# Delta-rule attention with a two-layer expert, float32 on one core: the front of the program reordered as a whole

## The chip, the cores and the metric

The kernel runs on one core of one Trainium2 chip. The metric is device time of one execution in microseconds (us). Three runs of the kernel before took 591.02 (median), 589.74 and 594.14 us.

## The reference, cut to what matters

```python
# q, k, v: (4 batches, 8 heads, 768 steps, 48); beta: (4, 8, 768)
k_n = k / (norm(k, axis=-1) + 1e-06)
for t in range(768):                       # state: 48 x 48 per head
    y[t] = q[t] @ state
    state += beta[t] * outer(k_n[t], v[t] - k_n[t] @ state)
x = y.transpose(0, 2, 1, 3).reshape(3072, 384)
h = x @ w_in                               # 384 x 2048
g = where(h >= 1, h, where(h <= -1, 0, (h + 1) ** 2 / 4))
return g @ w_out                           # 2048 x 384
```

## The kernel before, in words

**Tiling.** The 768 steps are cut into 12 chunks of 64, two chunks are a pair (G = 0 to 5), and all 32 heads of a chunk are worked on together. Inside a chunk the recurrence becomes a triangular system of 64 x 64 per head. For chunk g, `gram_k` makes the products of the keys with each other and `gram_q` those of queries and keys, of which only one triangle may stay (the mask). The systems of a pair are laid out one to a partition (`lanes`), scaled by beta and the squared norms of the keys, and inverted: `solve` does blocks of 16 x 16 on VectorE in 15 steps of a product and a subtraction, `unlanes` transposes the result back, and TensorE joins the blocks to 32 and 64 (`merge16_a`, `merge16_b`, `merge32`). The state is then carried from chunk to chunk by `chain_r` (correct the values by the old state), `chain_u` (apply the inverse), `chain_y` (the outputs y), and `chain_d` (the new state).

**The expert.** Its hidden width of 2048 is cut into 16 tiles f. `up` makes h for the 512 tokens of a pair (nine float32r products of 512 columns, since operands are split in a high and a low part and three of four combinations are kept), ScalarE and VectorE form g and split it (`rest`), and `down` adds g times the second weight into four banks. Each weight tile arrives packed and is unpacked once, in the first pair: `grow` and `cast` on ScalarE, `shift`, `join` and `low` on VectorE.

**Front and loop.** Nothing of the expert can start until the first chunk is through its chain. This front is the code from `load_k(0)` down to `spare[:] =`. After it, `items` runs over the pairs and tiles, with the attention work of later chunks threaded in. The first pair is done in halves at first: its first `HALF` = 6 items use chunk 0 alone (256 columns).

**What sets the order.** The order is written by hand (`manual_schedule`): each engine takes its instructions in the order of the code. Two tables of letters place small tasks: `FRONT`, one string for each stage of the front, and `FILL`, one for each item. A comma separates the points in a stage or item. `A` is the next ScalarE step of unpacking (`grow` or `cast`), `D` the next one of VectorE (`shift`, `join`, `low`), `L` the next step of the second pair's `lanes`, `S` one of its solve, `s`, `t` a scaling of values by key norms, `m`, `M` one mask product, `w` the load of the next weight tile, `F` one product of zeros by `dense` (TensorE gets work whose result is not used).

`stage` issues a stage's products, then the letters ahead of the comma, then the evictions:

```python
def stage(pieces, n):
    evicts = products(*pieces)
    codes = FRONT[n].split(",")
    do(codes[0])
    finish(evicts)
    do(codes[1])
```

Loads go out on SyncE's queue in the order of the code; at most eight of them are under way, since each waits for the one eight places ahead to have landed.

Of the kernel before, what the change touches and what calls it, by code (L numbers as in the profile page):

```python
# [19 lines left out]
DF = 2048  # L20
FT = DF // 128
WARM = 8
IDLE = 18
DENSE = (8, 4, 8, 10)
HALF = 6
PASSES = ((0, 0), (0, 1), (1, 0))
# [14 lines left out]
def delta_rule_moe(ctx: ExitStack, tc: tile.TileContext, kqa, kqb, kv, beta, w, out):  # L41
# [14 lines left out]
    nc = tc.nc  # L56
# [9 lines left out]
    const = ctx.enter_context(tc.tile_pool(name="const", bufs=1))  # L66
    sb = ctx.enter_context(tc.tile_pool(name="sb", bufs=2))
# [13 lines left out]
    def half(x):  # L81
        return slice(x * H, x * H + H)
# [38 lines left out]
    def weight_loads(n0, n1, q=nc.sync):  # L121
# [7 lines left out]
    beta_sb = const.tile([P, NS, 32], F32, name="beta_sb")  # L129
# [16 lines left out]
    for c0, base, step, n in ((0, -H, -C, NP), (NP, -C - H - NP, C, NP), (C, -C, C, H)):  # L146
        x = perm[:, 0:C].rearrange("c (a f l) -> c a f l", f=2, l=H)[:, :, :, c0:c0 + NP] if c0 < C else perm[:, C:P].rearrange("c (a f l) -> c a f l", f=2, l=H)
# [12 lines left out]
    nc.vector.memset(warm.bitcast(F32), 0.0)  # L160
    warm_ps = ps.tile([P, 512], F32, name="o1")

    def dense(n):
        for _ in range(n):
            nc.tensor.matmul(warm_ps, warm[:, 0:P], warm, start=True, stop=True)  # L165
    dense(WARM)
    mask = const.tile([P, C], F32, name="mask")
    nc.gpsimd.memset(mask, 1.0)
    for r in (0, C):
        nc.gpsimd.affine_select(out=mask[r:r + C], in_=mask[r:r + C], pattern=[[1, C]], base=0,  # L170
                                channel_multiplier=-1, compare_op=ALU.is_gt, fill=0.0)
# [59 lines left out]
    def gram_k(g):  # L231

        x, b_ = KE.pop(g) if g in KE else K[g], banks(C)
        for j in range(H):
            for e, f in quarters():
                k, o = x[f * C:f * C + D, e * H + j, :], (1 - e) * C
                nc.tensor.matmul(b_[f][o:o + C, j], k, k, start=True, stop=True)  # L237

        def evict():
            for f in range(2):  # L240
                nc.scalar.copy(out=(GE[g - 2] if g in (2, 3) else GG[:, g % 2])[:, half(f)], in_=b_[f])
        return evict

    def gram_q(g):

        x, b_ = Q[g], banks(C)
        for j in range(H):
            for e, f in quarters():
                r, o = slice(f * C, f * C + D), other(e, f) * C
                nc.tensor.matmul(b_[e][o:o + C, j], K[g][r, e * H + j, :], x[r, (1 - f, 1)[e], e * H + j, :], start=True, stop=True)  # L250

        def moved():
            for o in range(2):
                yield x[o * C:o * C + C, o, 0:H], b_[0][o * C:o * C + C], slice(o * C, o * C + C)
            yield x[:, 0, H:NU], b_[1], slice(0, P)

        def evict():
            def raw():
                for a, b, r in moved():
                    nc.scalar.copy(out=a, in_=b)  # L260

            def masks(copied=False):
                for a, b, r in moved():
                    nc.vector.tensor_tensor(out=a, in0=a if copied else b, in1=mask[r, None, :].broadcast_to([r.stop - r.start, H, C]), op=ALU.mult)
                    yield

            def later():
                raw()
                for a, b, r in moved():
                    for c in range(r.start, r.stop, C):  # L270
                        y = x[c:c + C, 0 if r.stop - r.start > C else c // C, (0, H)[r.stop - r.start > C]:(H, NU)[r.stop - r.start > C]]
                        nc.gpsimd.affine_select(out=y, in_=y, pattern=[[0, H], [1, C]], base=0, channel_multiplier=-1,  # L272
                                                compare_op=ALU.is_gt, fill=0.0)
            return (raw, masks(True)) if g < 2 else lambda: run(masks()) if g < 4 else later()
        return evict

    def norms(n, out):

        y = sb.tile([P, 32], F32, name="y0")
        r = sb.tile([P, 32], F32, name="r1")  # L280
        nc.scalar.activation(out=y, in_=n, func=AF.Sqrt, bias=tiny)
        nc.vector.reciprocal(out=r, in_=y)
        nc.vector.tensor_tensor(out=r, in0=r, in1=n, op=ALU.mult)
        nc.vector.tensor_tensor(out=r, in0=r, in1=y, op=ALU.add)
        nc.vector.tensor_scalar(out=out, in0=r, scalar1=0.5, scalar2=1e-6, op0=ALU.mult, op1=ALU.add)
        return r

    def scale_v(g):

# [5 lines left out]
    S = {}  # L295
    ZT = XT[:, :, :, 0:32]

    def lanes(G):

        for g in range(2):  # L300
            x = GE[g] if G == 1 else GG[:, g]
            for u in (half(0), half(1)) if (G, g) == (0, 1) else (slice(0, NU),):
                for r in (0, C):
                    (nc.scalar.copy if G else nc.vector.tensor_copy)(out=x[r:r + 32, u, 32:64], in_=x[r:r + 32, u, 0:32])
            if G == 1:
                nc.scalar.copy(out=GD[:, g], in_=x[:, :, 32:64])
            yield
# [6 lines left out]
                nc.gpsimd.memset(Xf[:, 256 * s:256 * s + 256:17], 1.0)  # L314
        if G == 0:
            nc.gpsimd.memset(ZT[:, :, :, 16:32], 0.0)
        nc.vector.transpose(out=A, in_=(GD if G == 1 else GG[:, :, :, 32:64]).rearrange("p g u t -> p t (g u)"))
        yield
        n = sb.tile([P, 32], F32, name="N2")
        r = norms(A.rearrange("l j t -> l (j t)")[:, 0:1024:33], n)  # L320
        gm = S["gm"] = sb.tile([P, 32], F32, name="gm")
        nc.vector.reciprocal(out=r, in_=n)
        nc.vector.tensor_tensor(out=gm, in0=r, in1=beta_sb[:, G, :], op=ALU.mult)
        nc.vector.tensor_tensor(out=gm, in0=gm, in1=r, op=ALU.mult)
        N = S["N", G] = sb.tile([P, 32], F32, name="N3")
        if G:
            nc.vector.transpose(out=N, in_=n)
        yield
        if G >= WHOLE:
# [9 lines left out]
        if G == 0:  # L339
            nc.vector.transpose(out=N, in_=n)  # L340
        yield

    def solve(G):

# [297 lines left out]
    def run(gen, n=99):  # L642
        for _ in range(n):
            if next(gen, 0) == 0:
                break
# [62 lines left out]
    tasks.update({"m": raws[0][1], "M": raws[1][1], "S": solve(1), "U": unlanes(1)})  # L708
# [241 lines left out]
```

## Time and profile before

| | |
|---|---|
| median of 3 runs | 591.02 us |
| the profiled execution | 590.3 us, span 588.6 us, 1.7 us around it |
| TensorE matmul busy | 569.0 us (97%) |
| VectorE, ScalarE, GpSimd busy | 405.2 (69%), 327.5 (56%), 54.5 us (9%) |
| mean granted clock of TensorE | 0.992 of full speed |
| first product of the expert | starts at 51.00 us |

PE is TensorE, PEld its weight loads, DVE VectorE, ACT ScalarE, POOL GpSimd, SP SyncE. A row names line, engine, operation, output <- input, shape, and in brackets the idle time ahead of it and what ended that. "issue" is waiting for nothing that the profile shows.

### The profile page before, as it was taken

To read this page: it belongs to the slowest core of one execution; us is meant where nothing else is said; L and a number is where in the kernel's file an instruction comes from. 1 tells how busy PE (TensorE), PEld (TensorE's weight loads), DVE (VectorE), ACT (ScalarE), POOL (GpSimd) and SP (SyncE) were. 2 spreads that over 40 slices of the span, in tenths; PEclk is the share of its full clock that TensorE was granted. 3 is DMA by queue.
4 is the path that set the end of the run, shared out by engine and by line. 5 is a ranking of instruction groups with operands and counts; after the bars stand their busy time and mean duration, and the time that the engine had idled before them with its cause. 6 is when DMAs were issued, how large, how long until landed. Compare 5 with 4: busy or idle time off the path is not lost.

```text
span 588.6 us, 21697 instructions
## 1 busy us (share of the span) xinstructions
PE 569.0 (97%) x9585; PEld 493.3 (84%) x9585; DVE 405.2 (69%) x828; ACT 327.5 (56%) x587; POOL 54.5 (9%) x91
## 2 busy tenths in 40 slices
PE   8998899999999999999999999999999999999996
PEld 7776788788978888888888888888888888898986
DVE  5977999963689864599954599954599955333332
ACT  4648886358644575545575445575445564454443
POOL 6200010000000500010400011300011300000000
PEclk9979999999999999999999999999999999999999
DMA  5673766200333111134011134011133000020001
GB/s 147 199 253 138 213 212 192 77 4 10 95 81 100 31 32 39 39 97 114 24 33 41 37 103 119 16 30 45 36 106 96 1 3 16 15 55 1 0 2 53
DMA packets 32302, 42.77 MB, mean 73 GB/s; under 512 B 7056, under 2 KB 26768, under 8 KB 32208
## 3 DMA queue, kind: packets, MB, share of 16 engines
q1 hardware_dynamic: 31216, 40.41, 24.0%
q8 instruction: 75, 1.23, 0.9%
q0 software_dynamic: 576, 0.57, 0.4%
q10 hardware_dynamic: 416, 0.39, 0.2%
q14 instruction: 19, 0.16, 0.1%
HBM read 34.47 MB, written 4.72 MB: 67 GB/s over the span
## 4 chain that ended last, share of the span: by engine, by line
PE 47%; issue 22%; DVE 14%; DMA 6%; SPq 6%; ACT 2%; POOL 1%; POOLq 0%; DVEq 0%; ACTq 0%
PE h L738 18%; PE o L753 17%; DMA wt<-in_w_dram 4%; PE ch L534 3%; PE ch L237 2%; DVE s L893 2%; PE ch L508 2%; DVE pr L366 1%; DVE A L368 1%; DVE glo L857 1%; PE ch L250 1%; SPq L595 1%; PE ch L492 1%; DMA KV<-in_kv_dram 1%; DVE wt L208 1%
## 5 line engine op out<-in xcount | busy, mean ns | idle before, releaser
L738 PE MATMUL h<-xb,wt 128*128 128x512 f32 (+1 forms) x918 | 223.0, 386 | 5.1 <-DVE s L893 2.0
L753 PE MATMUL o<-wt,ghi 128*128 128x384 f32 x768 | 200.0, 342 | 0.1
L738 PEld LDWEIGHTS h<-xb,wt 128*128 128x128 f32 x918 | 161.8, 188 | 38.9 <-DVE s L893 3.4
L753 PEld LDWEIGHTS o<-wt,ghi 128*128 128x128 f32 x768 | 137.2, 188 | 7.0 <-issue 0.3
L753 PE MATMUL o<-wt,glo 128*128 128x384 f32 x384 | 129.4, 337 | 0.4 <-DVE glo L857 0.4
L856 ACT CAST ghi<-s 128x512 fp32r<-128x512 f32 (+1 forms) x102 | 60.8, 597 | 120.4 <-DVE s L893 107.8
L893 DVE SCALAR_TENSOR_TENSOR s<-s,h 128x512 f32<-128x512 f32 (+1 forms) x102 | 66.3, 650 | 77.1 <-ACT s L891 76.8
L877 ACT ACTIVATE s<-h,half 128x512 f32<-128x512 f32 (+1 forms) x102 | 67.4, 661 | 53.8 <-PE h L738 53.6
L857 DVE TENSOR_TENSOR glo<-s,ghi 128x512 fp32r<-128x512 f32 (+1 forms) x102 | 66.8, 654 | 39.5 <-ACT ghi L856 39.3
L753 PEld LDWEIGHTS o<-wt,glo 128*128 128x128 f32 x384 | 72.1, 188 | 1.0 <-DVE glo L857 1.0
L891 ACT ACTIVATE s<-s 128x512 f32<-128x512 f32 (+1 forms) x102 | 62.2, 610 | 2.2
L368 DVE TENSOR_TENSOR A<-A,pr 128x30 f32<-128x30 f32 (+14 forms) x120 | 45.4, 378 | 4.4
L366 DVE TENSOR_TENSOR pr<-A 128x30 f32<-128x30 f32 (+14 forms) x120 | 43.4, 362 | 2.2
L272 POOL TENSOR_SCALAR_AFFINE_SELECT Q<-Q 64x512 f32<-64x512 f32 x32 | 21.7, 680 | 117.4 <-ACT Q L260 116.0
L165 PE MATMUL o<-wx 128*128 128x512 f32 x87 | 27.8, 464 | 1.5 <-DVE tiny L175 1.5
L534 PEld LDWEIGHTS ch<-Q,SU 64*64 64x64 f32 (+3 forms) x1056 | 22.4, 135 | 3.7 <-ACT ghi L856 1.5
L534 PE MATMUL ch<-Q,SU 64*64 64x64 f32 (+3 forms) x1056 | 24.7, 222 | 0.0
L331 POOL TENSOR_SCALAR_AFFINE_SELECT A<-A 128x1024 f32<-128x1024 f32 x4 | 5.6, 1390 | 191.5 <-DMA xb<-X 148.1
L165 PEld LDWEIGHTS o<-wx 128*128 128x128 f32 x87 | 18.2, 220 | 5.6 <-DVE tiny L175 1.5
L626 DVE TENSOR_TENSOR SU<-ch,SU 48x384 f32<-48x384 f32 x36 | 19.9, 554 | 3.9 <-PE ch L607 3.5
L590 DVE TENSOR_TENSOR X<-ch,X 128x128 fp32r<-128x128 f32 x20 | 5.8, 292 | 23.5 <-ACT xb L586 22.5
L517 ACT COPY SU<-ch 64x384 f32<-64x384 f32 (+1 forms) x30 | 14.3, 476 | 7.0 <-PE ch L508 6.7
(168 smaller groups left out, 559.5 us busy)
## 6 DMA issues: line engine op xcount, KB each, us to landing
wt<-in_w_dram SPq DMA_DIRECT2D x16, 768.0 KB, 5.6
out_dram<-wx SPq DMA_DIRECT2D x44, 96.0 KB, 2.2
KV<-in_kv_dram SPq DMA_DIRECT2D x36, 96.0 KB, 2.4
KV<-in_kv_dram SPq DMA_DIRECT2D x72, 48.0 KB, 2.3
KV<-in_kv_dram SPq DMA_DIRECT2D x12, 192.0 KB, 2.7
xb<-X SPq DMA_DIRECT2D x60, 32.0 KB, 2.0
K<-in_kqb_dram SPq DMA_DIRECT2D x12, 128.0 KB, 2.6
Q<-in_kqb_dram SPq DMA_DIRECT2D x12, 128.0 KB, 2.7
```

What stands on the lines that cost most here:

```text
L165: nc.tensor.matmul(warm_ps, warm[:, 0:P], warm, start=True, stop=True)
L272: nc.gpsimd.affine_select(out=y, in_=y, pattern=[[0, H], [1, C]], base=0, channel_multiplier=-1, compare_op=ALU.is_gt, fill=0.0)
L366: nc.vector.tensor_tensor(out=pr, in0=A[:, 0:n, j:j + 1].broadcast_to([P, n, m]), in1=A[:, j:j + 1, j + 1:32].broadcast_to([P, n, m]), op= ...
L368: nc.vector.tensor_tensor(out=A[:, 0:n, j + 1:32], in0=A[:, 0:n, j + 1:32], in1=pr, op=ALU.add)
L534: nc.tensor.matmul(yy[i][o * C:o * C + C, e, p], SF[rows, u:u + C], w_[rows, x, k, :], **how)
L738: nc.tensor.matmul(h[:, cols(bs)], WT[f][:, 0, x, k * P:(k + 1) * P], XB[G][:, y, k, cols(bs)], start=(n == 0), stop=(n == 8))
L753: nc.tensor.matmul(oacc[G, k], (ghi, glo)[x][:, k * P:(k + 1) * P], WT[f][:, 1, y, :], start=(new and n == 0), stop=(left[G, b] == 0 and n ...
L856: nc.scalar.copy(out=ghi[:, c], in_=s[:, c])
L857: nc.vector.tensor_tensor(out=glo[:, c], in0=s[:, c], in1=ghi[:, c], op=ALU.subtract)
L877: nc.scalar.activation(out=s[:, c], in_=h[:, c], func=AF.Relu, bias=mid, scale=0.5)
L891: nc.scalar.activation(out=s[:, c], in_=s[:, c], func=AF.Square)
L893: nc.vector.scalar_tensor_tensor(out=s[:, c], in0=s[:, c], scalar=1.0, in1=h[:, c], op0=ALU.min, op1=ALU.max)
```

## The change

It touches the front, the twelve mask products of chunks 0 to 3, and five weight loads; all products of the expert and of the chain stay.

- **First norms.** The first pair's scale, beta / (norm + 1e-6)^2, was made by a square root on ScalarE, a Newton step, and two reciprocals. Now `squares` makes it from n + 2e-6 sqrt(n) + 1e-12 with one reciprocal; the norm itself, which scales the values, follows later (`norms_first`). Of the first four evictions of `gram_k` two go to VectorE, and two of its lane copies to ScalarE.
- **Masks.** All products with the mask tile on VectorE become selects on GpSimd, as chunks 4 to 11 have them. Those of chunks 0 and 1 stand behind two memsets in the front. Chunks 2 and 3 get a copy on ScalarE ahead of their selects.
- **Second pair's lanes** (transpose, norms, scaling) move to later places of VectorE's queue.
- **Loads.** The values of chunk 1 go ahead of weight tiles 2 to 4. Tiles 2 to 6 each get a `gate`, one element set by VectorE, behind which the load has to wait.
- **Products of zeros.** Ahead of the first merge 38 of 280 columns stand instead of 18 of 512; between the stages 5, 5, 5, 5 and 4 instead of 1, 12, 2, 5 and 3. The names of accumulators are dealt in another order, so that the first `up` no longer shares a bank with `chain_d`.

```diff
-IDLE = 18
+IDLE = 38
 FRONT = (
-    "sAwFALs,", "FLFFFDFFLFFFFF,F", "FFDD,S", "mFFFFFmm,", "AFFFD,AAw", ",", "DA,Dt")
+    "AFFFFFA,", "FFFFF,sswD", "FFFFF,D", "FFFFF,wDL", "AFFFF,AwD", "Dw,", "LLAw,ASDt")
...
+            if gate:
+                nc.vector.memset(RAW[f][0:1, 0, 0:1], 0.0)
             q.dma_start(out=RAW[f].bitcast(I32), in_=w.bitcast(I32)[:, f])
...
     load_kv(0)
-    weight_loads(2, 5)
     load_kv(1)
...
-            return (raw, masks(True)) if g < 2 else lambda: run(masks()) if g < 4 else later()
+            return (raw, select) if g < 2 else later
...
+    def squares(n, gm, out):
+        y = sb.tile([P, 32], F32, name="y0")
+        d = sb.tile([P, 32], F32, name="r1")
+        nc.scalar.activation(out=y, in_=n, func=AF.Sqrt, bias=tiny)
+        nc.vector.tensor_scalar(out=gm, in0=n, scalar1=1e-12, scalar2=None, op0=ALU.add)
+        nc.vector.tensor_copy(out=d, in_=n)
+        nc.vector.scalar_tensor_tensor(out=gm, in0=y, scalar=2e-6, in1=gm, op0=ALU.mult, op1=ALU.add)
+        nc.vector.reciprocal(out=gm, in_=gm)
+        nc.vector.tensor_tensor(out=gm, in0=gm, in1=beta_sb[:, 0, :], op=ALU.mult)
+        S["first"] = y, d, out
...
-    dense(IDLE)
+    dense(IDLE, 280)
...
     for x in (SF, SZ):
         nc.gpsimd.memset(x, 0.0)
+    for _, select in raws:
+        select()
     run(unlanes(0))
+    norms_first()
```

**VectorE between the first solve and the first merge.** Before, from the end of `unlanes` (the transposes into `XT`) to the subtraction that ends `merge16_b` (`XT<-XT,ch`), with the second pair's norms between:

```order
L394 STREAM_TRANSPOSE XT<-A 128x16x32
L396 STREAM_TRANSPOSE XT<-A 128x16x32
...
L317 STREAM_TRANSPOSE A<-wt_144 128x1024
...
L282 RECIPROCAL r_694<-y_693 128x32
...
L338 TENSOR_TENSOR A_712<-A,gm 128x256 x2
L424 TENSOR_TENSOR XT<-XT,ch 128x16x16
L425 STREAM_TRANSPOSE GG<-XT 128x16x32
```

The changed program there:

```order
L411 STREAM_TRANSPOSE XT<-A 128x16x32
L413 STREAM_TRANSPOSE XT<-A 128x16x32
L272 RECIPROCAL r_559<-y_462 128x32
L273 TENSOR_TENSOR r_559<-r_559,r_463 128x32
L274 TENSOR_TENSOR r_559<-r_559,y_462 128x32
L275 TENSOR_SCALAR N_458<-r_559 128x32
L358 STREAM_TRANSPOSE N_460<-N_458 128x32
L441 TENSOR_TENSOR XT<-XT,ch 128x16x16
L442 STREAM_TRANSPOSE GG<-XT 128x16x32
```

The second pair's transpose and norms have left this place; five small steps of the first pair's own norm stand there.

**VectorE around the first product of the expert.** Before, between the low part of y (`xb<-ch,xb`) and the work that follows (`KV` is the scaling of values, `wt<-xb,wt` is `low`):

```order
L561 TENSOR_TENSOR xb<-ch,xb 128x3x64 x2
L208 TENSOR_TENSOR wt_860<-xb,wt_860 128x2x384
L195 TENSOR_SCALAR xb<-xb 128x768
L292 TENSOR_TENSOR KV<-KV,N_461 128x384 x2
```

The changed program there:

```order
L578 TENSOR_TENSOR xb<-ch,xb 128x3x64 x2
L272 RECIPROCAL r_965<-y_964 128x32
...
L339 STREAM_TRANSPOSE N_815<-N_813 128x32
L350 TENSOR_TENSOR A_975<-A,gm 128x256 x2
L125 MEMSET wt_980 1x1
L372 TENSOR_TENSOR pr<-X,A_975 128x30
L374 TENSOR_TENSOR X<-X,pr 128x2x15
L191 TENSOR_SCALAR xb<-xb 128x768
L301 TENSOR_TENSOR KV<-KV,N_460 128x384 x2
```

The second pair's norms and scaling now come here; `low` of tile 0 has moved ahead of the first row.

**GpSimd in the front of the changed program** (`A`, `SU` and `wt` are buffers set to zero):

```order
L368 MEMSET A 128x1024
L719 MEMSET SU 128x1552
L719 MEMSET wt_165 128x1536
L262 AFFINE_SELECT Q<-Q 64x512 x8
L321 MEMSET X 128x512
```

The row of eight selects is new; before, the memset of `X` followed the two memsets.

## Rows read from the trace of the kernel before

**Rows 1.** The page's part 1: busy us (share of span) xinstructions.

```profile
PE 569.0 (97%) x9585; PEld 493.3 (84%) x9585; DVE 405.2 (69%) x828; ACT 327.5 (56%) x587; POOL 54.5 (9%) x91
```

**Rows 2.** Windows: busy us of PE, PEld, DVE, ACT, POOL, then PEclk, DMA, GB/s.

```profile
30.00:31.00 1.00, 0.71 (x52) 0.72 (x56) 1.00 (x2) 0.31 (x1) 0.00 (x0) 0.51 0.78 197
36.00:37.00 1.00, 1.00 (x3) 0.46 (x2) 0.97 (x4) 0.00 (x0) 0.00 (x0) 0.57 1.03 302
...
55.00:60.00 5.00, 3.92 (x200) 3.47 (x200) 5.00 (x9) 4.97 (x9) 0.00 (x0) 1.00 0.23 61
```

**Rows 3.** Timeline of DVE in the front: start us, us, instruction, [idle before].

```profile
7.96 2.24 DVE L304 COPY GG<-GG 32x512 f32<-32x512 f32 x6 [4.31 <-ACT GG L241]
10.23 2.01 DVE L317 STREAM_TRANSPOSE A<-GG 128x1024 f32<-128x1024 f32 x1
...
15.45 0.19 DVE L355 TENSOR_TENSOR pr<-X,A 128x30 f32<-128x30 f32 x1
...
24.21 0.43 DVE L391 TENSOR_TENSOR A<-X,gm 128x256 f32<-128x256 f32 x1
...
27.41 1.05 DVE L396 STREAM_TRANSPOSE XT<-A 128x512 f32<-128x512 f32 x1
...
31.07 0.35 DVE L282 RECIPROCAL r<-y 128x32 f32<-128x32 f32 x1
...
33.45 0.76 DVE L338 TENSOR_TENSOR A<-A,gm 128x256 f32<-128x256 f32 x2
34.12 0.42 DVE L424 TENSOR_TENSOR XT<-XT,ch 128x256 f32<-128x256 f32 x1
```

**Rows 4.** Timeline of PE in the front and the first items.

```profile
21.57 4.38 PE L165 MATMUL o<-wx 128*128 128x512 f32 x18
...
28.60 0.43 PE L419 MATMUL ch<-wt,XT 32*32 32x16 f32 x28 [0.75 <-ACT wt L412]
30.29 1.57 PE L419 MATMUL ch<-wt,XT 32*32 32x16 f32 x100 [1.26 <-issue]
31.79 5.35 PE L165 MATMUL o<-wx 128*128 128x512 f32 x12
37.07 1.20 PE L436 MATMUL h<-XT,GG 32*32 32x32 f32 x64
...
42.05 1.15 PE L508 MATMUL o<-KV,XT 64*64 64x48 f32 x64
...
48.18 0.31 PE L539 MATMUL ch<-Q,wt 64*64 64x64 f32 x5 [1.47 <-issue]
...
62.00 1.20 PE L436 MATMUL ch<-XT,GG 32*32 32x32 f32 x64 [0.53 <-DVE XT L424]
```

**Rows 5.** Timeline of POOL in the front, and in pair 2.

```profile
16.36 1.40 POOL L702 MEMSET SU<- 128x1552 f32 x1
...
285.99 2.89 POOL L272 TENSOR_SCALAR_AFFINE_SELECT Q<-Q 64x512 f32<-64x512 f32 x4 [4.69 <-ACT Q L260]
```

**Rows 6.** Timeline of DVE: one subtraction alone, and one beside those selects.

```profile
198.75 0.22 DVE L368 TENSOR_TENSOR A<-A,pr 128x30 f32<-128x30 f32 x1
...
288.23 0.71 DVE L368 TENSOR_TENSOR A<-A,pr 128x30 f32<-128x30 f32 x1
```

**Rows 7.** Timeline of DVE around the first items.

```profile
49.18 0.62 DVE L561 TENSOR_TENSOR xb<-ch,xb 128x192 fp32r<-128x192 f32 x2 [1.57 <-ACT xb L556]
49.72 0.95 DVE L208 TENSOR_TENSOR wt<-xb,wt 128x768 fp32r<-128x768 f32 x1
...
55.53 0.95 DVE L208 TENSOR_TENSOR wt<-xb,wt 128x768 fp32r<-128x768 f32 x1
...
61.53 0.42 DVE L424 TENSOR_TENSOR XT<-XT,o 128x256 f32<-128x256 f32 x1
```

**Rows 8.** Waits of PE, 50 to 150 us: us in total, times, longest.

```profile
PE h L738 <- DVE s L893: 2.0, 3, 1.1
```

**Rows 9.** The chain that ended last, in order of time: start, us, what.

```profile
29.67 9.21 DMA wt<-in_w_dram
```

More of the change, by code (lines that the diff above doesn't have):

```diff
@@ L161, in delta_rule_moe, with dense @@
     warm_ps = ps.tile([P, 512], F32, name="o1")
-    def dense(n):
+    def dense(n, cols=512):
         for _ in range(n):
-            nc.tensor.matmul(warm_ps, warm[:, 0:P], warm, start=True, stop=True)
+            nc.tensor.matmul(warm_ps[:, 0:cols], warm[:, 0:P], warm[:, 0:cols], start=True, stop=True)
     dense(WARM)
[L167 to L171, printed above, removed]
     mid = const.tile([P, 1], F32, name="half")
@@ L240, in evict @@
             for f in range(2):
-                nc.scalar.copy(out=(GE[g - 2] if g in (2, 3) else GG[:, g % 2])[:, half(f)], in_=b_[f])
+                (nc.vector.tensor_copy if f and g < 2 else nc.scalar.copy)(out=(GE[g - 2] if g in (2, 3) else GG[:, g % 2])[:, half(f)], in_=b_[f])
         return evict
@@ L260, in raw, with select @@
                     nc.scalar.copy(out=a, in_=b)
[L262 to L268, printed above, removed]
+            def select():
                 for a, b, r in moved():
@@ L273, in later, with newton @@
                                                 compare_op=ALU.is_gt, fill=0.0)
-            return (raw, masks(True)) if g < 2 else lambda: run(masks()) if g < 4 else later()
-        return evict
+            def later():
+                raw()
+                select()
+            return (raw, select) if g < 2 else later
+        return evict
+    def newton(r, n, y, out):
+        nc.vector.reciprocal(out=r, in_=y)
+        nc.vector.tensor_tensor(out=r, in0=r, in1=n, op=ALU.mult)
+        nc.vector.tensor_tensor(out=r, in0=r, in1=y, op=ALU.add)
+        nc.vector.tensor_scalar(out=out, in0=r, scalar1=0.5, scalar2=1e-6, op0=ALU.mult, op1=ALU.add)
     def norms(n, out):
@@ L281, in norms @@
         nc.scalar.activation(out=y, in_=n, func=AF.Sqrt, bias=tiny)
[L282 to L285, printed above, removed]
-        return r
+        newton(r, n, y, out)
+        return r
+    def squares(n, gm, out):
[8 more added lines that the diff above has]
+        S["first"] = y, d, out
     def scale_v(g):
@@ L303, in lanes @@
                 for r in (0, C):
-                    (nc.scalar.copy if G else nc.vector.tensor_copy)(out=x[r:r + 32, u, 32:64], in_=x[r:r + 32, u, 0:32])
+                    (nc.scalar.copy if G or u == half(0) else nc.vector.tensor_copy)(out=x[r:r + 32, u, 32:64], in_=x[r:r + 32, u, 0:32])
             if G == 1:
@@ L316, in lanes @@
             nc.gpsimd.memset(ZT[:, :, :, 16:32], 0.0)
+        n = sb.tile([P, 32], F32, name="N2")
+        diag = A.rearrange("l j t -> l (j t)")[:, 0:1024:33]
+        gm = S["gm"] = sb.tile([P, 32], F32, name="gm")
+        N = S["N", G] = sb.tile([P, 32], F32, name="N3")
         nc.vector.transpose(out=A, in_=(GD if G == 1 else GG[:, :, :, 32:64]).rearrange("p g u t -> p t (g u)"))
         yield
[L319 to L326, printed above, removed]
+        if G == 0:
+            squares(diag, gm, n)
+        else:
+            r = norms(diag, n)
+            nc.vector.reciprocal(out=r, in_=n)
+            nc.vector.tensor_tensor(out=gm, in0=r, in1=beta_sb[:, G, :], op=ALU.mult)
+            nc.vector.tensor_tensor(out=gm, in0=gm, in1=r, op=ALU.mult)
             nc.vector.transpose(out=N, in_=n)
@@ L338, in lanes, with norms_first @@
             nc.vector.tensor_tensor(out=A16[:, s], in0=A[:, b, b], in1=gm[:, b, None].broadcast_to([P, 16, 16]), op=ALU.mult)
-        if G == 0:
-            nc.vector.transpose(out=N, in_=n)
         yield
+    def norms_first():
+        y, d, n = S["first"]
+        r = sb.tile([P, 32], F32, name="r1")
+        newton(r, d, y, n)
+        nc.vector.transpose(out=S["N", 0], in_=n)
     def solve(G):
@@ L659, in delta_rule_moe @@
     spare += START
-    acts = [(f, grow) for f in range(2)] + [x for f in range(FT) for x in ((f + 2, grow), (f, cast)) if x[0] < FT]
+    acts = [(f, grow) for f in range(2)] + [x for f in range(FT) for x in (((f + 2, grow), (f, cast)) if f > 1 else ((f, cast), (f + 2, grow))) if x[0] < FT]
     vecs = [x for f in range(FT + 1) for x in ((f, shift), (f, join), (f - 1, low)) if 0 <= x[0] < FT]
@@ L702, in delta_rule_moe @@
         nc.gpsimd.memset(x, 0.0)
+    for _, select in raws:
+        select()
     run(unlanes(0))
+    norms_first()
     one_ = lambda f, *a: [lambda: f(*a)]
@@ L707, in delta_rule_moe @@
     stage(one_(merge16_b, 0), 1)
-    tasks.update({"m": raws[0][1], "M": raws[1][1], "S": solve(1), "U": unlanes(1)})
+    tasks.update({"S": solve(1), "U": unlanes(1)})
     stage(one_(merge32, 0, None, True), 2)
@@ L713, in delta_rule_moe @@
     stage(both(chain_d, 0), 6)
-    spare[:] = START[0:2] + START[4:6]
+    spare[:] = START[0:4]
     oacc, gs = {}, {}
```

12 lines of the change are left out of this document (6 added, 6 removed).

## The prediction, made before the changed kernel ran

> **What bounds the kernel now.** The page's engine line comes first: TensorE is busy for 569.0 of 588.6 us [rows 1]. The rest, some 20 us, is ahead of the first product of the expert or in holes, so the time is the moment when the first `up` starts (51.00 us, the table) plus what TensorE then loses. Second, the timeline of TensorE in the front [rows 4]: there most of its "busy" is products of zeros, so the busy share says nothing about whether the front can be shorter. Third, what the real products wait for: lanes, the solve (15.45 to 24.21), `unlanes` (to 27.41 + 1.05 = 28.46), all on VectorE [rows 3], then merges and chain. Fourth, the windows: from 55 to 60 us VectorE is busy 5.00 of 5 us and TensorE 3.92 [rows 2]. So in the first items, too, VectorE sets the pace, and work that the change puts on it there is paid in full.
>
> **The change part by part.**
>
> *Norms and lanes.* The six lane copies cost VectorE 2.24 us, 0.37 each [rows 3]. Two go to ScalarE, two evictions come the other way; halves that run beside each other gain me 0.6 us (an estimate; bounds 0 and the two copies' 0.75). From the end of the transpose (10.23 + 2.01 = 12.24) to the solve's first step are 3.2 us of small steps [rows 3]. A reciprocal (0.35, as the second pair's) and about four steps of 0.2 with their turns go: 1.2 us, bounds 0 and 2.0. The solve then starts at 15.45 - 1.8 = 13.7.
>
> *Masks.* Eight selects on GpSimd now follow the two memsets. One memset took 1.40 us beside the solve [rows 5]; after two of them from about 14 us the selects start near 17.3 and last 8 x 2.89/4 = 5.8 us [rows 5], so they fall inside the solve. This is the part that speaks against the change: one subtraction of the solve took 0.22 us alone and 0.71 beside such a select [rows 6]. A step of the solve comes on average every (24.21 - 15.45)/30 = 0.29 us. In 5.8 us go 5.8/0.72 = 8 slowed steps, which need 8 x 0.29 = 2.3 us otherwise: 3.4 us are lost. Bounds: 0, if the selects are late enough to miss the solve, and 8 x (0.71 - 0.22) = 3.9; I take 3.4, as rows 6 show this pair of operations itself. The solve ends at 13.7 + 8.8 + 3.4 = 25.9, `unlanes` (28.46 - 24.21 = 4.25) at 30.1, later than before.
>
> *First merge.* `merge16_b` started 0.15 us after `unlanes` and worked 0.43 + 1.57 us, with a hole of 1.26 between [rows 4]. Now it runs from 30.25 to 32.25. Behind it, before, the subtraction waited on VectorE until 34.12 behind the second pair's transpose, norms and scaling [rows 3], and `merge32` until 37.07 behind twelve products of zeros, 5.35 us at about half of the clock [rows 4, 2]. Both covers go: subtraction and transpose (0.42 and about 0.7) end near 33.4, five products of 280 columns cost 5 x 280/6144 x 5.35 = 1.2 us beside them. `merge32` starts at about 33.45: **+3.6 us**. The 38 products ahead of it are 10640 columns for 9216, 4.38 x 1.155 = 5.1 us from 21.57, so they end near 26.7 and stand ahead of nothing that could run. They would matter only if the selects cost nothing: `merge16_b` could not start before 28.2, so at most 2.1 more is to be had there. Between the later stages 1400 columns replace 1024 to 2560: nothing, since the evictions they cover are unchanged.
>
> *The two holes.* Inside `merge16_b` TensorE stood 1.26 us, inside `chain_y` 1.47 us, with "issue" [rows 4]: no semaphore, hence no cause in the profile. Both stand where weight tiles stream (0.78 to 1.03 of the DMA engines busy [rows 2]). The values now come first and tiles singly, so I expect the second hole nearly gone, **+1.0** (bounds 0 and 1.47), and the first to return in part, **-0.4** (0 and -1.26). The Trainium skill, "Runtime: NRT & Kernel Launch", section "Instruction fetch mechanics", says that an engine's sequencer fetches its next block of instructions while it executes, and that this is mostly hidden. By that rule neither hole is late instructions that lighter loads would bring sooner, and no row here shows which it is; that outcome is the third rival.
>
> *VectorE after y.* The second pair's norms (31.07 to 33.45 without the 0.5 of a `shift`: 1.9), its scaling (0.76) and two solve steps (0.4) now follow y at once, where `low` of tile 0 (0.95 [rows 7]) stood: 1.9 + 0.76 + 0.4 - 0.95 = 2.1. Before, from y's last piece to the second pair's merge subtraction passed 61.53 - 49.80 = 11.7 us of a full VectorE [rows 7, 2]. So that subtraction, and with it the second pair's `merge32`, comes later against y: **-2.1** (bounds -1.2, if the solve steps and part of the scaling merely move, and -3).
>
> *A hole ahead of that merge.* `low` of tile 2 ended at 56.48 and `merge32` began at 62.00, with TensorE filling what lay between [rows 7, 4]. With `low` earlier, its products are through and TensorE stands, by about 5.5 less 0.8 for the rest of the item, 4.7 us. The wait itself is in the term before. But after TensorE had stood for most of 27.8 to 30.3 us, its clock at 30 us was 0.51, the lower level of 1.2 GHz, and at 36 still 0.57 [rows 4, 2]. So it ran about six microseconds at half. If it falls again I take **-2.3**: six microseconds at half clock lose at most 3.2, but VectorE is the bound for part of them. Bounds 0 and -3.2.
>
> *Later waits.* TensorE waited three times for VectorE's `s` in the first items, 2.0 us together [rows 8]. These go when unpacking is less bunched: **+1.9** (0 and 2.0).
>
> *Loads and gates.* Five one-element memsets are nothing on VectorE. Queued on SP behind each gate are the next tiles and then the later chunks' loads, needed tens of microseconds on. When tile 2 lands is a rival.
>
> **Sum.** 3.6 - 0.4 + 1.0 - 2.1 - 2.3 + 1.9 = 1.7 us gained. Against the profiled execution, 590.3, that is 588.6. The median of the three runs is 0.7 above it, the lowest 0.6 below; I add 0.3 and forecast **588.9 us**. With all terms at their ends the sum goes from about -4 to +7, but ends do not coincide.
>
> **Rivals.**
>
> *(a) VectorE's crowding costs less.* The clock stays up in the hole (TensorE still works in it, as it did from 55 to 60 us), or the selects miss the solve. For it: 0.71 is one subtraction's duration, and the memset beside the solve slowed nothing [rows 5, 3]. Against: rows 6 are this very pair. The first gives 588.9 - 2.3 = 586.6, the second 588.9 - 2.1 = 586.8, both 584.5. Chance 0.30.
>
> *(b) Slower: a late tile 2.* Its gate comes after the first merge and two scalings of values, about 34.5 us, and ScalarE's `grow` of it stands in the queue ahead of the evictions of `chain_y`, due near 44 (48.18 less 3.2 and 1.0). `grow` takes 0.9, so it costs time as soon as the tile needs over 43.1 - 34.5 = 8.6 us from its issue, and every microsecond beyond delays y and all that follows. For it: one weight tile took 9.21 us [rows 9]; the DMA engines were full at 36 us [rows 2]. Against: then several tiles shared the engines, now tiles go singly. At 13 us the price is 4.4: 593.3, slower than before; above 10.5 us the gain is gone. Chance 0.10.
>
> *(c) The holes stay.* Both "issue" holes return whole: 1.0 lost in `chain_y`, 0.9 more in `merge16_b`, so the gain is -0.2 and the time 590.8, no change. For it: nothing in the profile ties them to loads but the place. Against: there are stretches of as many instructions without one. Here the change does not do what its order of loads says. Chance 0.18; by the rule of the Trainium skill above it would be the likeliest for `chain_y`.
>
> **How the numbers follow.** Forecast 0.42 (587.5 to 590.2), (a) 0.30 (584 to 587.5), (c) 0.18 (590.2 to 592), (b) 0.10 (592 to 597). The range 584.8 to 592.5 leaves out the quickest tenth and most of (b). What a measurement can tell from no change is 1%, 5.9 us: faster is below 585.1, which only the lower end of (a) reaches with a little from the forecast's other bounds, 0.15; slower is above 596.9, (b)'s far end, 0.05; within 1%, 0.80.
>
> **What would show it.** In the profile after: subtractions and products of the solve at 0.7 us beside selects from about 17 to 23 us, and 0.2 before and behind (right for the mask term; at 0.2 throughout it falls); `merge32` at about 33.5 and `chain_u` 3 us earlier than 42.05; the first `up` near 47 us; a wait of TensorE for `XT` of 4 to 5 us ahead of the second pair's `merge32`, near 60 us, and a granted clock of 0.5 in the windows behind it; no hole inside `chain_y`; no wait of TensorE for `s` in the first items. Wrong it is if `grow` of tile 2 waits for a load, if a new "issue" hole of over 1 us opens in the front, or if the first `up` comes early and the end does not follow, since then the loss lies in the items and not in the terms above.

## The result: slower by 1.3%, and the profile after

Four runs of the changed kernel took 597.92 us (median; 596.64 to 603.07), four of the kernel before (the three named above and one more) 592.58. The ratio is **1.0127** (1.0086 to 1.0168): some 7.5 us slower by the ratio (the two medians alone are 5.3 us apart), where 1.7 us faster was forecast and 592.5 was the range's end. The profiled execution took 599.1 us, span 597.4, mean granted clock 0.974 (before 590.3, 588.6, 0.992). Runs of one kernel spread by up to 10 us here, so times are compared by ratios to the kernel before, each with its 95% interval; a trace says where time lies in one execution.

`s` is VectorE's step in forming g, one for each item, so its times tell how far the expert has come. The first is 4.9 us later than before (58.61 for 53.73), and the fourteenth still 4.5. The fifteenth is 9.2 later, and the last 8.8: a second loss falls near 125 us. The windows show both. Columns are busy us of PE, PEld, DVE, ACT, POOL, then granted clock, DMA share, GB/s.

```profile
30.00:35.00 5.00, 4.85 (x136) 3.72 (x135) 2.40 (x9) 1.21 (x3) 0.00 (x0) 0.52 0.35 93
35.00:40.00 5.00, 4.62 (x71) 3.20 (x70) 4.94 (x11) 1.17 (x3) 0.00 (x0) 0.50 0.73 224
40.00:45.00 5.00, 5.00 (x73) 3.78 (x71) 0.59 (x1) 1.87 (x4) 0.00 (x0) 0.50 0.38 145
45.00:50.00 5.00, 4.90 (x101) 3.68 (x101) 2.37 (x7) 1.99 (x4) 0.00 (x0) 0.77 0.11 12
...
60.00:65.00 5.00, 5.00 (x158) 4.52 (x160) 4.65 (x8) 3.16 (x6) 0.00 (x0) 0.57 0.30 99
120.00:125.00 5.00, 4.27 (x180) 3.21 (x168) 3.59 (x7) 3.40 (x7) 0.00 (x0) 1.00 0.20 57
125.00:130.00 5.00, 3.09 (x10) 3.09 (x11) 2.64 (x5) 1.05 (x2) 0.00 (x0) 0.58 0.02 3
130.00:135.00 5.00, 5.00 (x79) 3.76 (x79) 0.00 (x0) 2.15 (x4) 1.42 (x3) 0.74 0.00 0
```

TensorE runs at 1.2 GHz from 30.2 to 47.3 us, where before it came back at 36.9 [rows 2]; and twice more in the expert, from 57.5 to 64.3 and from 125.8 to 132.6. On VectorE the steps of the solve, the end of `unlanes`, the first merge's subtraction and the second pair's:

```profile
17.63 0.29 DVE L372 TENSOR_TENSOR pr<-X,A 128x126 f32<-128x126 f32 x1
17.96 0.71 DVE L374 TENSOR_TENSOR X<-X,pr 128x126 f32<-128x126 f32 x1
...
23.02 0.68 DVE L372 TENSOR_TENSOR pr<-X,A 128x110 f32<-128x110 f32 x1
23.73 0.28 DVE L374 TENSOR_TENSOR X<-X,pr 128x110 f32<-128x110 f32 x1
...
29.37 1.04 DVE L413 STREAM_TRANSPOSE XT<-A 128x512 f32<-128x512 f32 x1
...
33.91 0.42 DVE L441 TENSOR_TENSOR XT<-XT,ch 128x256 f32<-128x256 f32 x1 [2.43 <-PE ch L436]
...
66.85 0.41 DVE L441 TENSOR_TENSOR XT<-XT,o 128x256 f32<-128x256 f32 x1
```

Eight steps take 0.68 to 0.71 us beside the selects, and 0.3 just before and behind them. The timeline of TensorE answers to [rows 4]:

```profile
28.06 1.59 PE L422 MATMUL ch<-XT,GG 32*32 32x16 f32 x128 [0.71 <-DVE XT L411]
29.59 2.01 PE L166 MATMUL o<-wx 128*128 128x512 f32 x5
...
31.97 1.89 PE L436 MATMUL ch<-wt,XT 32*32 32x16 f32 x124 [0.15 <-issue]
33.79 2.08 PE L166 MATMUL o<-wx 128*128 128x512 f32 x4
36.25 0.80 PE L166 MATMUL o<-wx 128*128 128x512 f32 x1 [0.39 <-issue]
36.98 1.92 PE L453 MATMUL o<-XT,GG 32*32 32x32 f32 x64
...
45.53 1.92 PE L525 MATMUL h<-KV,XT 64*64 64x48 f32 x64
...
52.69 1.23 PE L758 MATMUL h<-xb,wt 128*128 128x256 f32 x9
...
54.86 1.23 PE L422 MATMUL ch<-XT,GG 32*32 32x16 f32 x125 [0.78 <-issue]
...
58.59 1.65 PE L166 MATMUL o<-wx 128*128 128x512 f32 x3 [1.59 <-issue]
...
67.32 0.88 PE L453 MATMUL ch<-XT,GG 32*32 32x32 f32 x42 [0.50 <-DVE XT L441]
...
126.91 0.69 PE L773 MATMUL o<-wt,ghi 128*128 128x384 f32 x1 [2.18 <-issue]
```

`merge32` starts where it did before (36.98 for 37.07), `chain_u` 3.5 us later, the first `up` 1.7 later, the second pair's `merge32` 5.3 later. Two holes (idle stretches of TensorE) of 1.59 and 2.18 us, marked issue, each stand at the start of a stretch at half clock.

**What issue is.** The page's part 3 has a queue for instructions:

```profile
q8 instruction: 75, 1.23, 0.9%
```

75 packets of 16 KB, while TensorE ran 9606 weight loads, 9606 products and 147 other instructions: 258 each. Counted in the order in which TensorE started them, the first instruction behind the holes of 1.59 and 2.18 us lies within one of number 194 + 256 n, and so does the first one behind each of the 55 issue holes of 0.5 us or more in the fourteen traces of this study. I call these numbers borders, and border 19 is the one with n = 19. In the changed kernel border 19 is passed at 123.10 us. The window 123.1 to 124.5 of the DMA view has nothing but one packet, at its very end:

```profile
DMA packets 1, 0.02 MB, mean 12 GB/s; under 512 B 0, under 2 KB 0, under 8 KB 0
...
q8 instruction: 1, 0.02, 3.9%
```

It takes 0.9 us, and TensorE goes on 1.5 us after it has landed. Where the packet starts 0.9 to 1.8 us after its border, as this one does, a hole ends 3.4 to 4.3 us after that border. Of the 55 holes 44 end 3.4 us or more after the border before; in the other eleven, 2.2 to 3.1 us, the packet started within 0.7 us of that border or ahead of it. Without a hole, too, borders can lie closer (1.8 us once in this trace), where the packet had started ahead. A merge of 128 products is a whole such piece and takes 1.2 us. Where a second merge or other small products followed at once, TensorE stood at the border.

### The profile page after: what moved, and what is told of

The parts are those of the page before. It is cut to its first block, busy times and chain, and to the rows that moved or that the text cites. A ratio compares the mean times of both kernels' runs of the same rounds, so it can differ in the third digit from the quotient of the medians.

```text
span 597.4 us, 21784 instructions
## 1 busy us (share of the span) xinstructions
PE 578.6 (97%) x9606; PEld 501.3 (84%) x9606; DVE 404.1 (68%) x823; ACT 330.9 (55%) x593; POOL 65.5 (11%) x104
## 4 chain that ended last, share of the span: by engine, by line
PE 54%; issue 23%; DVE 14%; ACT 3%; DMA 3%; SPq 1%; POOL 1%; POOLq 0%; DVEq 0%; ACTq 0%
PE h L758 19%; PE o L773 17%; PE ch L551 3%; PE o L166 3%; PE ch L233 2%; PE ch L509 2%; DMA wt<-in_w_dram 2%; DVE A L385 1%; DVE pr L383 1%; PE ch L525 1%; PE ch L246 1%; DVE s L913 1%; DVE glo L877 1%; DVE SU L643 1%; DMA Q<-in_kqb_dram 1%
## 5 line engine op out<-in xcount | busy, mean ns | idle before, releaser
L262 POOL TENSOR_SCALAR_AFFINE_SELECT Q<-Q 64x512 f32<-64x512 f32 x48 | 33.5, 698 | 163.0 <-ACT Q L256 160.8
L166 PE MATMUL o<-wx 128*128 128x512 f32 (+1 forms) x108 | 31.6, 439 | 3.5 <-issue 2.0
L166 PEld LDWEIGHTS o<-wx 128*128 128x128 f32 x108 | 20.6, 222 | 8.0 <-issue 3.1
L256 ACT COPY Q<-ch 64x512 f32<-64x512 f32 (+1 forms) x33 | 19.2, 582 | 8.5 <-PE ch L246 7.8
```

The costliest lines, as they stand in the source:

```text
L166: nc.tensor.matmul(warm_ps[:, 0:cols], warm[:, 0:P], warm[:, 0:cols], start=True, stop=True)
```

## The experiments

**Fewer instructions, the same zeros (e1_wide).**

```diff
-IDLE = 38
+IDLE = 21
-    dense(IDLE, 280)
+    dense(IDLE)
```

> The changed kernel with 21 products of zeros of 512 columns ahead of the first merge in place of 38 of 280 (10752 columns for 10640), so 17 products, 34 TensorE instructions, fewer and nothing else. Theory (instruction supply): in both traces every 256th TensorE instruction is a border, borders never lie closer than 3.4 us, and each hole marked issue of over 0.3 us ends at one; fewer instructions ahead move the borders against the work. The 2.18 us hole at 124.7 us then shrinks to 0.5 or less, the half clock behind it (125.8 to 132.6) does not come, and the hole of 1.59 us at 57 shrinks to about 1: 3 to 5 us faster than the changed kernel, ratio to before about 1.005. Rival (the holes are late loads or chance): the holes stay where they are, same time as the changed kernel, ratio 1.013.

Measured: 594.23 us, ratio 1.0050 (1.0016 to 1.0085), 0.8% below the changed kernel. The hole and the half clock at 125 us are gone:

```profile
125.00:130.00 5.00, 5.00 (x207) 4.48 (x206) 4.69 (x8) 2.55 (x5) 0.00 (x0) 1.00 0.03 8
130.00:135.00 5.00, 5.00 (x83) 4.28 (x83) 2.26 (x2) 4.46 (x8) 4.08 (x7) 1.00 0.02 5
```

34 instructions less ahead of 26 us decide over a hole at 125 us, with the loads and the columns of zeros as good as unchanged. So a late load did not make it. The holes near 57 us shrank less than they moved: 0.52, 0.78 and 1.03 us at 53.8, 57.6 and 61.6, and in this execution (596.6 us) the clock fell behind them, from 63.1 to 76.8. The least distance of borders in the expectation, 3.4 us, holds at six of the seven holes of its two traces (2.35 us at the last), and not at every border.

**More instructions in the kernel before (e2_narrow).**

```diff
-IDLE = 18
+IDLE = 42
-    dense(IDLE)
+    dense(IDLE, 220)
```

> The kernel before with 42 products of zeros of 220 columns in place of 18 of 512 (9240 columns for 9216): 24 products, 48 TensorE instructions, more, and nothing else. Theory (instruction supply): that puts the borders where the changed kernel has them in the four merges between 106 and 122 us, so a new hole of about 2 us comes near 120 us in the products of down, with the clock at half for some 6 us behind it: 3 to 5 us slower than before, ratio 1.006 to 1.009. Rival (holes belong to loads or to chance): ratio 1.000, no hole there.

Measured: 595.37 us, ratio 1.0075 (1.0048 to 1.0101). TensorE's holes:

```profile
36.65 3.78 PE L165 MATMUL o<-wx 128*128 128x512 f32 x8 [2.49 <-issue]
...
124.69 0.44 PE L753 MATMUL o<-wt,ghi 128*128 128x384 f32 x1 [1.36 <-issue]
```

48 more instructions of zeros alone make the kernel before slower by more than half of what the change does. The hole came where forecast (1.36 us, without half clock behind it), but most of the loss lies ahead of `merge32`, which comes 3.3 us later (40.36): at 36.65 a border falls among the twelve products of zeros, while weight tiles fill the DMA engines, and half clock lasts to 41.0. 6.2 us lie between that border and the one before. So the size came out as forecast in good part by luck.

**Products of zeros between the stages, short (e3_tiny).**

```diff
-    "AFFFFFA,", "FFFFF,sswD", "FFFFF,D", "FFFFF,wDL", "AFFFF,AwD", ...
+    "AfffffA,", "fffff,sswD", "fffff,D", "fffff,wDL", "Affff,AwD", ...
+            elif c == "f":
+                dense(1, 8)
```

> The changed kernel with the products of zeros between the stages cut to 8 columns (23 of them; their number and so all borders stay). Theory (at half clock from 30.2 to 47.3 us each such product takes 0.5 us and stands ahead of the next stage): chain_u comes 4 to 6 us earlier than 45.53, near 40 to 41, first up near 48; what is left of it at the end depends on VectorE and on the clock, which I expect to come back no earlier in time than before: 2 to 4 us faster than the changed kernel. Rival (they only fill the time of evictions): chain_u within 1 us of 45.5 and the same time. Second rival (without them the clock stays low far into the items): chain_u early but the end 2 us or more later.

Measured: 596.04 us, ratio 1.0091 (1.0059 to 1.0124), which the intervals do not tell from the changed kernel's.

```profile
36.37 0.38 PE L166 MATMUL o<-wx 128*128 128x8 f32 x1 [1.44 <-issue]
...
43.40 2.06 PE L525 MATMUL h<-KV,XT 64*64 64x48 f32 x64
```

`chain_u` came at 43.4 us, 2.1 earlier and not 4 to 6; the first `up` at 51.9, 0.8 earlier. Holes of 0.94 and 1.44 us opened in the place of the zeros (32.1 and 36.4 us), and the clock came back only at 50.1. The 24 products of zeros mostly filled time that the borders take anyway.

**Selects out of the solve (e4_selects).**

```diff
             nc.gpsimd.memset(X, 0.0)
+            if G == 1:
+                for _, select in raws:
+                    select()
...
-    for _, select in raws:
-        select()
     run(unlanes(0))
```

> The changed kernel with the eight selects of chunks 0 and 1 behind the memset of X on GpSimd, which waits for the solve's result, so that they run beside transposes instead of beside the solve. Theory: no step of the solve over 0.3 us, solve 3.3 us shorter (ends near 22.8), unlanes near 27.1; but the 38 products of zeros end at 26.9 and now stand ahead of the first merge, so merge16_b comes only about 1.5 us earlier (30.0 for 31.5), and without TensorE's wait of 0.7 us at 27.3 the clock may hold: 1 to 4 us faster than the changed kernel. Rival (selects are not what delays the front): merge16_b within 0.5 us of 31.5 and the same time.

Measured: 592.44 us, ratio 1.0024 (0.9991 to 1.0056): 1.0% below the changed kernel, at least as much as forecast. No step of the solve is over 0.3 us, it ends at 22.6, and the clock is at half from 32.5 to 39.3 only. Windows, then TensorE:

```profile
35.00:40.00 5.00, 5.00 (x95) 3.91 (x90) 2.19 (x2) 1.42 (x3) 0.00 (x0) 0.57 0.72 241
40.00:45.00 5.00, 4.90 (x114) 3.80 (x114) 2.68 (x7) 3.63 (x6) 0.00 (x0) 1.00 0.46 168
```

```profile
47.37 1.22 PE L759 MATMUL h<-xb,wt 128*128 128x256 f32 x9
...
49.81 1.23 PE L425 MATMUL ch<-XT,GG 32*32 32x16 f32 x125 [1.05 <-issue]
...
54.63 1.65 PE L166 MATMUL o<-wx 128*128 128x512 f32 x3 [2.70 <-issue]
```

The first `up` is 5.3 us earlier than in the changed kernel and 3.6 earlier than before. Within 8 us two holes of 3.75 us together, and half clock from 53.0 to 59.8 behind them, eat the lead.

**Zeros dealt as before (e5_twelve).**

```diff
-    "AFFFFFA,", "FFFFF,sswD", "FFFFF,D", ...
+    "AFA,", "FFFFFFFFFFFF,sswD", "FF,D", ...
```

> The changed kernel with its 24 products of zeros between the stages dealt out as 1, 12, 2, 5 and 4 in place of 5, 5, 5, 5 and 4. Theory (the clock stayed at half from 30.2 to 47.3 us because small groups of them stood between merges; in the kernel before twelve in a row stood at 31.8 to 37.1 and it rose at 36.9): it rises near 38 to 40 us, merge32 comes at about 38.4 in place of 37.0, but from there to chain_u 5.0 us in place of 8.6: chain_u near 43.4 for 45.5, first up near 50.6 for 52.7; the end follows by 1 to 2 us. Rival (the clock's return does not hang on how they are dealt): half clock until 45 us or later, first up within 0.7 us of 52.7.

Measured: 597.25 us, ratio 1.0107 (1.0064 to 1.0150).

```profile
39.02 1.20 PE L453 MATMUL o<-XT,GG 32*32 32x32 f32 x64
...
44.01 1.22 PE L525 MATMUL h<-KV,XT 64*64 64x48 f32 x64
...
50.37 1.22 PE L758 MATMUL h<-xb,wt 128*128 128x256 f32 x9
```

The clock rose at 38.5, `merge32` to `chain_u` took 5.0 us in place of 8.55, and the first `up` is at 50.4 as forecast. The intervals do not show that the end followed: in the trace, holes at 52.3, 55.7 and 127.3 us and half clock at 55.5 to 76.0 took the lead back.

**Norms and scaling earlier, on top of e4_selects (e6_norms).**

```diff
-    ... "AFFFF,AwD", "Dw,", "LLAw,ASDt")
+    ... "ALLFFFF,AwD", "Dw,", "Aw,ASDt")
```

> e4_selects, and the second pair's norms and scaling moved from behind y to the stage of chain_u, where VectorE stands idle for several us. Theory (the second pair's merge subtraction waits behind full VectorE, term of 2.1 us): from y's last piece to that subtraction 2 us less than in e4_selects, first s about 2 us earlier; the time about 1 to 2 us below e4_selects, ratio to before 0.999 to 1.001. Rival (TensorE's instruction borders are the bound there, 3.8 us apart and more beside weight loads): VectorE's steps come earlier, but the holes at 49 and 52 us stay and grow, and the time stays within 0.7 us of e4_selects.

Measured: 596.66 us, ratio 1.0092 (1.0061 to 1.0123), slower than e4_selects. The first `s` came 2.0 us earlier, as forecast; then a hole opened, inside a stretch of half clock from 52.1 to 76.0:

```profile
55.85 1.65 PE L166 MATMUL o<-wx 128*128 128x512 f32 x3 [4.08 <-issue]
```

**Thirteen wide products ahead of the first merge, on top of that (e7_thirteen).**

```diff
-IDLE = 38
+IDLE = 13
-    dense(IDLE, 280)
+    dense(IDLE)
```

> e6_norms with 13 products of zeros of 512 columns ahead of the first merge in place of 38 of 280 (25 products, 50 instructions, and about 1.4 us less). Theory (instruction supply): the first merge starts near 25.0 us in place of 26.3, and the borders move 50 instructions later in the work: the hole near 120 us (border 20) vanishes as in e1_wide, and near 50 us the two holes together shrink by over 1 us; 2 to 4 us faster than e6_norms, ratio to before 0.993 to 0.997. Rival (fewer products of zeros only let the clock fall earlier): the clock falls before 30 us and stays, the first up later than in e6_norms, no gain.

Measured: 591.97 us, ratio 1.0020 (0.9993 to 1.0046): 0.7% below e6_norms, but not the 0.993 to 0.997 forecast. The hole near 120 us is gone, but one of 3.2 us at 55.6 remained:

```profile
55.60 0.24 PE L512 MATMUL ch<-SU,K 48*64 48x48 f32 x1 [3.20 <-issue]
```

**Loads as before (e8_loads).** Weight tiles 2 to 4 go again ahead of the values of chunk 1, `w` stands in the first and fifth stage, and there is no gate.

> The changed kernel with the loads as before: weight tiles 2 to 4 ahead of the values of chunk 1, tiles 5 and 6 where before had them, no gates. Theory (the fetch of TensorE's next 256 instructions waits behind weight tiles in flight: in before the border at 42.2 us was followed by a fetch only at 45.9 and the hole in chain_y): the next fetch that falls beside the tiles starts 2 to 4 us after its border in place of 1.0, so a hole of 1 us or more in the front between 33 and 50 us, while the hole at 57 us, where no tiles fly then, shrinks. End within 2 us of the changed kernel either way. Rival (spacing is 3.8 us whatever the loads do): holes where the changed kernel has them and of the same size.

Measured: 601.10 us, ratio 1.0176 (1.0123 to 1.0230). The profiled execution took 604.95 us.

```profile
33.42 1.89 PE L437 MATMUL ch<-wt,XT 32*32 32x16 f32 x124 [1.13 <-issue]
38.79 0.80 PE L167 MATMUL o<-wx 128*128 128x512 f32 x1 [1.48 <-issue]
...
59.02 0.96 PE L167 MATMUL o<-wx 128*128 128x512 f32 x3 [0.78 <-issue]
```

As forecast, the holes went to where the tiles fly: the fetches start 2.9 and 2.6 us after their borders (28.1 and 33.4 us), and the hole at 57 us halves. The ratio is 0.5% (3 us) above the changed kernel's, but the two intervals overlap: that the loads' new order helped is likely and not shown.

**Tiles 2 to 5 in one burst, 6 and 7 after the first s (e9_tiles); norms behind y again (e10_behind).** Both stand on e7_thirteen, and tile 7 gets a gate too.

```diff
-    ... "FFFFF,sswD", "FFFFF,D", "FFFFF,wDL", "ALLFFFF,AwD", "Dw,", "Aw,ASDt")
+    ... "FFFFF,sswwwwD", "FFFFF,D", "FFFFF,DL", "ALLFFFF,AD", "D,", "A,ASDt")
-    "FtL,D,D,,,wADD", ...
+    "FtL,D,D,,,wwADD", ...
```

In e10_behind the letters LL stand in the last stage, as in the change.

> e7_thirteen with weight tiles 2 to 5 issued one behind the other after the first merge (near 34.5 to 36 us, landed by about 43) and tiles 6 and 7 only after the first s (near 51.6 us), so that none is in flight from 43 to 51 us. Theory (TensorE's instruction fetch starts about 1 us after a border, but 2 to 4 us after it beside weight tiles): border 8 near 49.3 us is followed by a fetch at 50.5 in place of 53.35, the hole of 3.2 us at 52.4 us shrinks to under 1, the half clock from 55.2 to 68.8 goes or is shorter: 3 to 6 us faster than e7_thirteen, ratio to before 0.992 to 0.997. Rival (VectorE bounds the first items): the hole goes, but TensorE waits as long for XT or s there, and the time stays within 1.5 us of e7_thirteen.

> e9_tiles with the second pair's norms and scaling behind y again, as the change has them. Theory (they stand on VectorE's path to the second pair's merge, 2.1 us in the prediction): from y's last piece to that pair's merge subtraction 1.5 to 2.5 us longer than in e9_tiles, and the time 1 to 2.5 us longer. Rival (TensorE is not waiting for VectorE there): that stretch longer, the time within 0.7 us.

Measured: 590.86 us, ratio 0.9998 (0.9969 to 1.0028), and 590.75, 1.0002 (0.9972 to 1.0031). In e9_tiles, with no tile in flight, the packet after border 8 starts 1.0 us behind it (47.84), where in e7_thirteen it started 4.06 us behind it (49.29). The hole at 55 us is gone (0.54 left), and, as the rival has it, VectorE is what TensorE waits for:

```profile
59.31 1.92 PE L456 MATMUL ch<-XT,GG 32*32 32x32 f32 x64 [2.95 <-DVE XT L444]
```

The gain on e7_thirteen, 0.2%, is below what the runs can tell. Where norms and scaling stand makes no difference of time that the runs show. Behind y, the stretch from y's last piece to the second pair's subtraction is 2.4 us longer, as forecast (15.0 for 12.6). Earlier, they hold up the copies behind `chain_u` (these start at 40.2 us, when `chain_u` had ended at 37.8), and y comes later by what was saved behind it, so that the subtraction stands at 58.9 and 58.7 us.

**VectorE's front in TensorE's order (e11_order), and all tiles in the burst (e12_burst).**

```diff
-    ... "FFFFF,sswwwwD", "FFFFF,D", "FFFFF,DL", "ALLFFFF,AD", "D,", "A,ASDt")
+    ... "FFFFF,ssLwwww", "FFFFF,L", "FFFFF,L", "FFFF,DDADA", "DD,", "A,ASDt")
```

The diff is against e9_tiles. e12_burst has six `w` there and none in the first item.

> e9_tiles with VectorE's queue in the front ordered by what TensorE waits for: the second pair's transpose, norms and scaling right after the first merge and ahead of the copies behind chain_u, the unpacking of tiles 0 and 1 behind those copies. In e9_tiles the copies started 2.4 us after chain_u ended (40.2 for 37.8), TensorE stood 1.6 us in chain_y, and its merge32 of the second pair waited 2.9 us for VectorE. Theory (the norms' gain of 2 us was given back there): copies within 0.3 us of chain_u's end, first up near 44.5 for 46.5, the second pair's merge32 2 us earlier: 1.5 to 3 us faster than e9_tiles, ratio to before 0.995 to 0.998. Rival (the instruction borders take it back: at 3.5 to 3.8 us each the stretch from y to the merge has no room): first up earlier, the end within 0.7 us of e9_tiles.

> e11_order with weight tiles 6 and 7 in the burst with 2 to 5 (from 34.4 us, landed by about 47) in place of near 51 us, so that no tile is in flight from 47 to 56 us. Theory (fetches beside tiles start 2 to 4 us after their border, alone about 1 us): after border 7 (44.2 us in e11_order) the spacings are 3.5 to 4 us, the hole of 3.0 us in the second pair's merge16_b at 54.8 us goes, and the half clock at 59.3 to 69.5 us goes or is shorter: 2 to 4 us faster than e11_order, ratio to before 0.993 to 0.997, faster than before. Rival (the loads only trade one hole for another: the burst now covers border 7 too): a hole of 2 us or more before 50 us, the time within 1 us of e11_order.

Measured: 590.32 us, ratio 0.9998 (0.9971 to 1.0024), and 589.20, **0.9968** (0.9937 to 0.9999). In e11_order the rival held: the first `up` came 0.45 us earlier, the ratio is that of e9_tiles. Tiles 6 and 7 were in flight when border 9 was passed at 51.9 us. The DMA view of 51.9 to 55.3 us has no instruction packet; the one behind it (55.3 to 56.3) has:

```profile
DMA packets 235, 1.35 MB, mean 396 GB/s; under 512 B 16, under 2 KB 16, under 8 KB 235
...
q1 hardware_dynamic: 235, 1.35, 97.5%
...
q8 instruction: 1, 0.02, 5.5%
```

and TensorE stands as long:

```profile
57.83 0.62 PE L439 MATMUL o<-wt,XT 32*32 32x16 f32 x52 [3.01 <-issue]
```

In e12_burst that hole is gone, and one of 2.93 us stands ahead of 50.3, since the burst now covers border 7: the rival's hole.

```profile
50.31 1.03 PE L425 MATMUL ch<-XT,GG 32*32 32x16 f32 x100 [2.93 <-issue]
```

But the half clock is down to 3.4 us (51.5 to 54.9). This version is faster than the changed kernel. It is also 0.3% below the kernel before, with an interval that just leaves out no change; as one of twelve such intervals, that is weak evidence.

## Why the prediction was wrong, point by point

Between the two traces the changed kernel is 1.7 us behind at the first `up`, where the sum had it 4 ahead, 4.9 at the first `s` and 9.2 at the fifteenth.

- **Solve and selects: right.** The solve started at 14.3 (13.7), eight steps were slowed by the factor forecast, `unlanes` ended at 30.4 (30.1). What was not priced is what the delay does next: without the selects beside the solve the half clock lasts 6.8 us in place of 17, and the kernel is 1.0% faster (e4_selects), some 6 us for a term of 3.4.
- **First merge, +3.6: the step that failed first.** `merge32` gained 0.1. The prediction took the five products between the stages as 280 columns wide, though only those ahead of the first merge are: by its own sum five of 512 columns are 2.2 us and not 1.2. And it did not see that five more stand between `merge16_a` and `merge16_b`, so that the latter started 1.1 us after `unlanes`. From 30.2 us on it all ran at half clock, 0.5 us a product of zeros. It also let the clock come back by itself and put the stages behind `merge32` at nothing: from `merge32` to `chain_u` took 8.55 us for 4.98 [rows 4]. So the first `up`, due near 47, came at 52.69. In e5_twelve, with twelve products in a row between the merges, the clock came back 9 us earlier; e3_tiny shows that shorter ones gain 0.8 us at the first `up`, since borders stand behind them and the clock comes back later still.
- **The holes, +1.0 and -0.4: right where they were, wrong where they went.** The one in `chain_y` is gone and the one in `merge16_b` is down to 0.15. But the sum took the holes as tied to loads at two places. They are tied to TensorE's instruction count (beside weight tiles they are longer), so a change that adds 20 products ahead of 26 us moves all borders behind them. New holes of 0.78, 1.59 and 2.18 us appeared, the last with 2.5 us more from half clock (9.2 less 4.5 less 2.18). e1_wide and e2_narrow show it from both sides, and so do all fourteen traces: the seven with 19359 instructions of TensorE (the changed kernel, e2 to e6, e8) have a hole of 0.62 to 2.18 us at border 20, near 122 to 132 us, and the seven with 19309 to 19325 (the kernel before, e1, e7, e9 to e12) have none there. The prediction's own signs of being wrong looked for a new hole of over 1 us in the front alone; here they opened behind the first `up`. The prediction weighed the Trainium skill, "Runtime: NRT & Kernel Launch", "Instruction fetch mechanics": fetching goes on during execution and is mostly hidden. By number the traces agree: of some 1050 borders in them 55 show a hole of 0.5 us or more. They disagree where small products follow one another: the packet starts about 1 us after a border, or 2 to 4 us beside weight tiles, and TensorE stands until 1.1 to 1.6 us after it has landed. The prediction drew from the rule only that the holes stay.
- **VectorE after y, -2.1:** the stretch from y's last piece to the second pair's subtraction grew from 11.7 to 14.4 us, 2.7 for the 2.1 forecast. Yet TensorE waited only 0.50 us for that subtraction, and with the work moved away the time is the same (e9_tiles, e10_behind): no run shows this term in the time.
- **Half clock behind the hole ahead of that merge, -2.3:** half clock came (57.5 to 64.3 us), but behind a hole at a border; the wait for XT was 0.50 us and not 4.7.
- **Later waits, +1.9:** TensorE's waits for `s` fell from 2.0 us [rows 8] to 1.5:

```profile
PE h L758 <- DVE s L913: 1.5, 3, 0.8
```

- **Rivals:** none of the three was it. Tile 2 was not late (ScalarE's `grow` of it waited for no load). A rival that moves holes, and not only keeps them, was missing; of those named only (b) ended on the slower side, and for another reason.

What stays open: why the clock falls behind some holes and not behind others of the same length (1.36 us in e2_narrow without, 1.59 us here with), and what exactly delays a fetch beside weight tiles. No run takes back by itself the first pair's norms, the masks of chunks 2 and 3, or the order of accumulators; e7_thirteen keeps all three and is within 0.5% of the kernel before.

## What to carry to other kernels

Where small products fill TensorE, count its instructions: here a stretch of 256 that ran in well under 3.4 us could end in a hole, and any edit ahead of it, were it only zeros, moved all later borders. A hole or a slowed step cost more than its length where TensorE's clock fell behind it, so price what it triggers too. Before a gain in the front is booked, look whether the stretch behind it has room to take it.

## What the runs showed of the hardware

- A TensorE instruction fetch was one packet of 16 KB for 256 instructions. It took 0.9 to 1.6 us; at the holes it started about 1 us after a border with quiet DMA engines (e9_tiles, border 8: 1.0) and up to 4.2 us after it while weight tiles were in flight (e12_burst, border 7).
- Adding 24 short products of zeros, 48 instructions, changed the time by 0.75% (e2_narrow).
- VectorE's two-input steps of 0.27 to 0.29 us (110 to 128 columns) took 0.68 to 0.71 us for as long as selects ran on GpSimd, as much as one of 30 columns took [rows 6]; memsets there did not slow them. In e4_selects a one-input step of 128 x 32, 0.18 us else, took 0.68 beside the selects as well (`N<-r` at 28.23).
